# One v block turned on TensorE, paced loads, idle products and shared last-token products in an attention-then-MLP kernel

## The chip, the cores and the metric

The kernel runs on one core of one Trainium2 chip. The metric is device time in microseconds (us), and each quoted figure is the median of several executions of one program.

## The reference

Four batches of 6080 tokens and 256 channels go through a channel attention (the 256x256 score matrix is over channels, not tokens) and then through a two-layer MLP with a tanh gelu:

```python
qn = q / (np.linalg.norm(q, axis=1, keepdims=True) + 1e-06)      # q, k, v: (4, 6080, 256) f32
kn = k / (np.linalg.norm(k, axis=1, keepdims=True) + 1e-06)
s = kn.transpose(0, 2, 1) @ qn / tau                             # (4, 256, 256)
a = softmax(s)                                                   # cut: max, exp, sum
x = (v @ a).reshape(24320, 256)
h = x @ w_in                                                     # (24320, 2048)
g = 0.5 * h * (1.0 + np.tanh(c * (h + 0.044715 * h * h * h)))
return g @ w_out                                                 # (24320, 256) f32
```

## The kernel before

Phase one reads q and k of batch 0, and builds the score matrix G and the column sums. A short head computes the softmax and folds the attention matrix into w_in (`aw` = a @ w_in), so that the MLP can work straight on v. Then come 48 blocks (12 a batch, 512 tokens each, the twelfth 448). Block n computes its first layer from the turned v block `vT` while PE also does the output products `yp` of block n-1, and, a slice at a time, the score products of the next batch:

```python
for i in range(NP):                                   # 8 steps a block
    hp = pH.tile([128, 2, 512], FP32, tag="h", name="hp")
    for j in range(2):
        fc = 2 * i + j
        for cc in range(2):
            nc.tensor.matmul(hp[:, j, :cols], lhsT=aw[:, cc, fc * 128 : fc * 128 + 128],
                             rhs=vT[:, cc, :cols], start=cc == 0, stop=cc == 1)
    nc.scalar.activation(g[:, 2 * i : 2 * i + 2, :cols], hp[:, :, :cols], AF.Gelu_apprx_tanh)
    ...                                               # cut: more_aw
    if before is not None:
        h = i % 2
        y_part(before, i // 2, h * NP, h * NP + NP)   # 8 output products of one slot of 128 tokens
    next(fill, None)                                  # a slice of the next batch's scores
```

v arrives by a load from GpSimd's queue, cast to bf16, and is turned by four DMA transposes from SyncE's queue, one for each slot of 128 tokens. Block 1 is turned ahead of the loop, every later block two blocks ahead:

```python
def turn_v(nb):
    t = v_of.pop(nb)
    ...
    for s in range(n):
        nc.sync.dma_start_transpose(out=vT[:, :, s * 128 : s * 128 + 128], in_=t[:, s, :])
...
    vT = vT_of.pop(nb)          # in the loop over blocks
    turn_v(nb + 2)
    load_v(nb + 4)              # five buffers for v
```

Before the first block the kernel asks for both weight matrices, v blocks 1 to 3 and the first three q/k pieces of batch 1, in one burst. The twelfth block of a batch has 448 tokens: three full slots and one of 64. The half slot takes as many output products (16) as a full one:

```python
nc.tensor.matmul(yp[:rows, at, :], lhsT=g[:, fc, s * 128 : s * 128 + rows],
                 rhs=wout_bf[:, fc, :], start=fc == 0, stop=fc == FC - 1)
```

## Time and profile before

| | before |
|---|---|
| median of 3 runs | 776.29 us (775.14 to 776.45) |
| profiled execution | 776.96 us, span 775.2 us, mean granted clock 0.989 |
| PE busy | 95% of the span |
| PE waits for the turned v of block 1 | 10.1 us |
| block 0, 1, 2, 3 start | 45.03, 64.59, 81.63, 97.26 us |
| an ordinary block, from start to start | 15.20 to 15.63 us while it also does score products (blocks beside a change of batch differ), 13.89 us where it doesn't |

A block's start is read throughout as the start of its first weight load on PE; its first product begins up to 0.3 us later. The span runs from the first to the last instruction; device time is 1.8 us more. Two lines of the page's costliest groups show how to tell a bound engine from a waiting one (busy and mean duration come ahead of the second bar, idle time and what ended most of it after it):

```profile
L488 ACT ACTIVATE g<-hp 128x1024 bf16<-128x1024 f32 (+1 forms) x384 | 389.6, 1015 | 327.1 <-PE hp L484 307.6
L262 POOL DMA_DIRECT2D vb<-in_v_dram x47 | 25.5, 543 | 213.0 <-DMA vT<-vb 204.7
```

ScalarE stood idle 307.6 us for PE's products, so it follows PE. GpSimd stood 204.7 us for transposes to land before it could ask for another v block, which costs nothing by itself: it sits on a queue far ahead of need. Only a wait of PE is time lost.

### The profile page before, as it was taken

The numbers are of one execution on the slowest core, as the hardware profiler recorded it, in microseconds if no ns is written. First come the engines' busy times: TensorE is split into PE (matmuls) and PEld (weight loads), VectorE is DVE, ScalarE is ACT, GpSimd is POOL, SyncE is SP. The second block draws the span as 40 slices with busy tenths as digits, with TensorE's granted clock in tenths as the row PEclk, the third lists the DMA queues.
The fourth block names the chain that finished last, engine by engine and source line by source line (L and its number), as shares of the span: only waits on it lengthen the run. The fifth ranks groups of instructions, "written<-read, shape, count | busy, mean of one in ns | idle before, by whom it ended". The sixth has DMA issues, their size and how long they took to land.

```text
span 775.2 us, 12214 instructions
## 1 busy us (share of the span) xinstructions
PE 739.3 (95%) x5155; PEld 507.8 (66%) x5240; DVE 277.9 (36%) x487; ACT 420.9 (54%) x413; POOL 65.2 (8%) x121
## 2 busy tenths in 40 slices
PE   4776999999999999999999999999999999999998
PEld 3534666666666666666667666666766666666666
DVE  4731454544521454544431264545351101110011
ACT  5752555555555555555545555555545555555552
POOL 0231011001210001000300010100100000000000
PEclk9987999999999999999999999999999999999999
DMA  9999568412983365721695167723432333212111
GB/s 367 319 193 174 105 127 144 82 41 63 187 140 82 76 126 99 149 52 41 119 173 112 38 130 133 132 55 78 85 69 80 67 69 89 60 50 74 40 55 52
DMA packets 82039, 83.86 MB, mean 108 GB/s; under 512 B 56640, under 2 KB 61504, under 8 KB 81984
## 3 DMA queue, kind: packets, MB, share of 16 engines
q0 software_dynamic: 17648, 32.97, 25.8%
q1 hardware_dynamic: 64048, 49.18, 23.7%
q8 instruction: 41, 0.67, 0.4%
q10 hardware_dynamic: 288, 0.92, 0.3%
q14 instruction: 14, 0.11, 0.0%
HBM read 78.91 MB, written 24.90 MB: 134 GB/s over the span
## 4 chain that ended last, share of the span: by engine, by line
PE 90%; DMA 6%; SPq 1%; issue 1%; ACT 1%; POOL 0%; DVE 0%; ACTq 0%; DVEq 0%
PE yp L432 44%; PE hp L484 41%; PE G L124 4%; DMA st<-in_k_dram 3%; DMA vT<-vb 2%; DMA vb<-in_v_dram 1%; PE ps L184 1%; SPq L276 0%; POOL win_bf L291 0%; ACT sqb L230 0%; SPq L78 0%; PE cols L136 0%; ACT g L488 0%; PE T L162 0%; DVE qkb L225 0%
## 5 line engine op out<-in xcount | busy, mean ns | idle before, releaser
L488 ACT ACTIVATE g<-hp 128x1024 bf16<-128x1024 f32 (+1 forms) x384 | 389.6, 1015 | 327.1 <-PE hp L484 307.6
L484 PE MATMUL hp<-vT,aw 128*128 128x512 bf16 (+1 forms) x1458 | 385.4, 378 | 14.0 <-DMA vT<-vb 10.1
L432 PE MATMUL yp<-wout_bf,g 128*128 128x256 bf16 (+1 forms) x3072 | 397.9, 273 | 0.8 <-issue 0.2
L432 PEld LDWEIGHTS <-g 128*128 128x128 bf16 (+1 forms) x3072 | 301.1, 98 | 114.7 <-issue 3.3
L484 PEld LDWEIGHTS <-aw 128*128 128x128 bf16 x1536 | 149.8, 98 | 117.9 <-issue 14.5
L449 DVE COPY ysb<-yp 128x512 f32<-128x512 f32 (+1 forms) x93 | 64.0, 689 | 402.7 <-PE yp L432 402.7
L373 DVE TENSOR_TENSOR acc<-acc,sq 128x512 f32<-128x512 f32 (+1 forms) x141 | 97.5, 692 | 4.8
L124 PE MATMUL G<-qkb 128*128 128x256 bf16 (+1 forms) x384 | 74.0, 296 | 14.9 <-DVE qkb L225 14.9
L372 DVE TENSOR_TENSOR sq<-qkb 128x512 bf16<-128x512 bf16 (+1 forms) x141 | 58.7, 417 | 0.0
L124 PEld LDWEIGHTS <-qkb 128*128 128x128 bf16 (+1 forms) x384 | 39.0, 105 | 23.4 <-DVE qkb L225 15.8
L262 POOL DMA_DIRECT2D vb<-in_v_dram x47 | 25.5, 543 | 213.0 <-DMA vT<-vb 204.7
L193 DVE TENSOR_SCALAR aw<-ps,rsinv 128x512 bf16<-128x512 f32 x30 | 22.4, 749 | 26.2 <-PE ps L184 21.2
L78 POOL DMA_DIRECT2D qkb<-in_q_dram x24 | 13.2, 549 | 203.0 <-PE G L124 119.3
L230 ACT ACTIVATE sqb<-st 128x3072 bf16<-128x3072 f32 (+5 forms) x10 | 21.1, 2123 | 10.6 <-DMA st<-in_k_dram 10.6
L225 DVE CAST qkb<-st 128x3072 bf16<-128x3072 f32 (+6 forms) x12 | 14.6, 1225 | 15.0 <-DMA st<-in_k_dram 15.0
L184 PE MATMUL ps<-win_bf,eT 128*128 128x512 bf16 x54 | 17.1, 394 | 0.1
L383 POOL TENSOR_TENSOR r<-r,half 128x4 f32<-128x4 f32 x3 | 3.1, 1038 | 142.1 <-DVE r L382 142.1
L78 POOL DMA_DIRECT2D qkb<-in_k_dram x24 | 13.2, 549 | 4.5 <-DMA wout_bf<-in_moe_w_out_dram 1.9
L408 DVE RECIPROCAL den<-den 128x256 f32<-128x256 f32 x6 | 10.5, 1753 | 0.2
L453 DVE COPY ysb<-yp 64x256 f32<-64x256 f32 (+1 forms) x7 | 2.7, 415 | 21.2 <-PE yp L432 21.2
L184 PEld LDWEIGHTS <-eT 128*128 128x128 bf16 x60 | 5.9, 101 | 2.5 <-issue 1.1
L212 DVE TENSOR_TENSOR pair<-sqb 128x1536 bf16<-128x1536 bf16 (+2 forms) x7 | 5.8, 836 | 0.0
(51 smaller groups left out, 66.5 us busy)
## 6 DMA issues: line engine op xcount, KB each, us to landing
out_dram<-ysb SPq DMA_DIRECT2D x44, 512.0 KB, 2.9
vb<-in_v_dram POOLq DMA_DIRECT2D x43, 256.0 KB, 5.6
qkb<-in_q_dram POOLq DMA_DIRECT2D x21, 384.0 KB, 6.0
qkb<-in_k_dram POOLq DMA_DIRECT2D x21, 384.0 KB, 8.0
st<-in_q_dram SPq DMA_DIRECT2D x5, 768.0 KB, 10.4
st<-in_k_dram SPq DMA_DIRECT2D x5, 768.0 KB, 12.1
vT<-vb SPq DMA_TRANSPOSE x188, 3.8
out_dram<-ysb SPq DMA_DIRECT2D x4, 384.0 KB, 2.4
```

Source lines behind the costliest of these rows:

```text
L78: engines[x].dma_start(out=dst[:, x, 0:size, :], in_=src[b, s0 * 128 : (s0 + size) * 128, :].rearrange("(p s) c -> p s c", s=size))
L124: nc.tensor.matmul(G[:, ic, :], lhsT=qk[:rows, 1, s, ic * 128 : ic * 128 + 128], rhs=qk[:rows, 0, s, :], start=first and ic == 0, stop=las ...
L184: nc.tensor.matmul(ps, lhsT=eT[:, jc, ic * 128 : ic * 128 + 128], rhs=win_bf[:, jc, fs * 512 : fs * 512 + 512], start=jc == 0, stop=jc == 1)
L193: nc.vector.tensor_scalar_mul(dst, ps, scale)
L230: nc.scalar.activation(sqb[:rows, :, lo:hi], st[:rows, :, lo:hi], AF.Square)
L262: nc.gpsimd.dma_start(out=t[:, 0:n, :], in_=v_rows[r0 : r0 + n * 128, :].rearrange("(p s) c -> p s c", s=n))
L372: nc.vector.tensor_mul(sq[:rows], flat, flat)
L373: nc.vector.tensor_add(acc[:rows], acc[:rows], sq[:rows])
L432: nc.tensor.matmul(yp[:rows, at, :], lhsT=g[:, fc, s * 128 : s * 128 + rows], rhs=wout_bf[:, fc, :], start=fc == 0, stop=fc == FC - 1)
L449: nc.vector.tensor_copy(ysb[:, s0 : s + 1, :], yp[:, 0 : s + 1 - s0, :])
L484: nc.tensor.matmul(hp[:, j, :cols], lhsT=aw[:, cc, fc * 128 : fc * 128 + 128], rhs=vT[:, cc, :cols], start=cc == 0, stop=cc == 1)
L488: nc.scalar.activation(g[:, 2 * i : 2 * i + 2, :cols], hp[:, :, :cols], AF.Gelu_apprx_tanh)
```

## The change

Its intent has three parts. First, get rid of the wait at block 1: turn that v block on PE during block 0, and ask for less in the first burst (v block 3 ahead of the second q/k piece; four v buffers, not five). Second, keep the PE clock up through the tail of phase one and the softmax head by products on a constant `filler` tile that nobody reads. Third, let the half-full last tokens of two batches share one set of 16 output products, and spread a block's output products evenly over its steps. The core of the diff (cuts are marked):

```diff
-    vin = ctx.enter_context(tc.tile_pool(name="vin", bufs=5))
+    vin = ctx.enter_context(tc.tile_pool(name="vin", bufs=4))
...                                # cut: the last two phase-one chunks reuse free halves of earlier staging buffers
+    def keep_clock(n):
+        for _ in range(n):
+            idle = pH.tile([128, 2, 512], FP32, tag="h", name="idle")
+            nc.tensor.matmul(idle[:, 0, :], lhsT=filler[:, 0:128], rhs=filler, start=True, stop=True)
...
+        if n >= TAIL - 2:         # phase one, chunk n of 11 (TAIL = 7)
+            keep_clock(size)
...
-    for n in range(3):
-        load_qk(1, n)
-        if n < 2:
-            load_v(n + 2)
+    load_qk(1, 0)
+    load_v(2)                     # the rest is asked for from block 0 on
...
+    keep_clock(5)                 # head, ahead of turning the scores
...
-        nc.scalar.activation(vT0[:, cc, :], vps[:, cc, :], AF.Copy)    # in the loop over cc
+    nc.scalar.activation(vT0, vps, AF.Copy)
+    keep_clock(1)
...
-    turn_v(1)
+    def turn_v_on_pe(nb):
+        ...
+        for cc in range(2):
+            for s in range(4):
+                nc.tensor.matmul(p[:, cc, s * 128 : s * 128 + 128],
+                                 lhsT=t[:, s, cc * 128 : cc * 128 + 128],
+                                 rhs=ident_bf, is_transpose=True)
+        nc.vector.tensor_copy(vT, p)
...
+        for n in range(10):
+            if n % 3 == 0 and n < 9 and (b, n // 3) not in loaded_of:
+                load_qk(b, n // 3)
+            if b == 1 and n == 5:
+                turn_v_on_pe(1)
             yield
...
-            load_v(nb + 4)
+            load_v(nb + 3)
+            if cols % 128:        # the half slot
+                if kept is not None:
+                    gr, row0 = kept
+                    nc.gpsimd.tensor_copy(g[:, :, cols : cols + rest], gr)
+                    now["rests"] = [(0, row), (rest, row0)]
+                    now["rows"] = now["rows"] + [2 * rest]
+                elif b + 1 < B:
+                    gr = grp.tile([128, FC, rest], BF16, tag="gr", name="gr")
+                    kept = (gr, row)
...
-                    h = i % 2
-                    y_part(before, i // 2, h * NP, h * NP + NP)
+                    todo = [(s, fc) for s in range(len(before["rows"])) for fc in range(FC)]
+                    for s, fc in todo[len(todo) * i // NP : len(todo) * (i + 1) // NP]:
+                        y_part(before, s, fc, fc + 1)
+            if cols % 128 and kept is not None:
+                nc.gpsimd.tensor_copy(kept[0], g[:, :, cols - rest : cols])
```

More of the change, by code (lines that the diff above doesn't have):

```diff
@@ L54 @@
     gp = ctx.enter_context(tc.tile_pool(name="gp", bufs=2))
-    vin = ctx.enter_context(tc.tile_pool(name="vin", bufs=5))
+    vin = ctx.enter_context(tc.tile_pool(name="vin", bufs=4))
+    grp = ctx.enter_context(tc.tile_pool(name="grp", bufs=1))
     pA = ctx.enter_context(tc.tile_pool(name="pA", bufs=2, space=bass.MemoryType.PSUM))
@@ L89 @@
     n_all = S_ALL + 1
-    first_chunks = chunks_of([2, 5, 6, 6, 6, 6, 6, 4, 3, 2, 1], 7)
-    TAIL = 7
+    first_chunks = chunks_of([2, 5, 6, 6, 6, 6, 6, 4, 3, 2, 1], 1)
+    TAIL, SHARED = 7, 9
     staged = []
@@ L97, in stage_chunk @@
         if n < len(first_chunks):
-            st = stage.tile([128, 2, SMAX, 256], FP32, tag="st", name="st")
+            if n < SHARED:
+                st = stage.tile([128, 2, SMAX, 256], FP32, tag="st", name="st")
+            else:
+                st = staged[n - 2][:, :, first_chunks[n - 2][1] :, :]
             load_chunk((nc.sync, nc.scalar if n < 2 else nc.sync), st, 0, first_chunks[n])
@@ L106 @@
     make_identity(nc, ident)
+    ident_bf = const.tile([128, 128], BF16)
+    nc.gpsimd.tensor_copy(ident_bf, ident)
+    filler = const.tile([128, 512], BF16)
+    nc.gpsimd.memset(filler, 1.0)
     ones_bf = const.tile([128, 1], BF16)
@@ L348 @@
     vT_of[0] = vT0
-    turn_v(1)
-    def attention_steps(b, aw_next):
-        if b > 1:
-            for n in range(3):
-                load_qk(b, n)
-        for _ in range(10):
+    def turn_v_on_pe(nb):
+        t = v_of.pop(nb)
+        vT = vts.tile([128, 2, 512], BF16, tag="vT", name="vT")
+        p = pA.tile([128, 2, 512], BF16, tag="a", name="vps")
+        for cc in range(2):
[4 more added lines that the diff above has]
+        nc.vector.tensor_copy(vT, p)
+        vT_of[nb] = vT
+    def attention_steps(b, aw_next):
+        for n in range(10):
[3 more added lines that the diff above has]
+                turn_v_on_pe(1)
             yield
@@ L446, in y_part @@
         s0 = s - at
-        n = sum(x == 128 for x in rows_of)
+        n = st["n"]
         if s < n:
@@ L456, in y_part @@
                 out=out[r0 : r0 + n * 128, :].rearrange("(p s) c -> p s c", s=n), in_=ysb[:, 0:n, :])
-        if s >= n:
-            nc.sync.dma_start(out=out[r0 + n * 128 : r0 + n * 128 + rows, :], in_=ysb[:rows, s, :])
+        for lo, row in st["rests"] if s >= n else []:
+            nc.sync.dma_start(out=out[row : row + rest, :], in_=ysb[lo : lo + rest, s, :])
+    rest = N % 128
+    assert rest <= 64
+    kept = None
     before = None
@@ L472 @@
             turn_v(nb + 2)
-            load_v(nb + 4)
+            load_v(nb + 3)
             g = gp.tile([128, FC, 512], BF16, tag="g", name="g")
+            n_full = cols // 128
             now = {
                 "b": b, "blk": blk, "g": g, "final": nb == B * n_blocks - 1,
-                "rows": [min(128, cols - s * 128) for s in range((cols + 127) // 128)],
+                "n": n_full, "rows": [128] * n_full, "rests": [],
             }
+            if cols % 128:
+                row = b * N + t0 + n_full * 128
+                if kept is not None:
[3 more added lines that the diff above has]
+                    now["rows"] = now["rows"] + [2 * rest]
+                    kept = None
+                elif b + 1 < B:
+                    gr = grp.tile([128, FC, rest], BF16, tag="gr", name="gr")
+                    kept = (gr, row)
+                else:
+                    now["rests"] = [(0, row)]
+                    now["rows"] = now["rows"] + [rest]
             for i in range(NP):
```

## The prediction

> **What bounds the kernel now.** I read the page first (engine shares, then the chain that ended last), then busy time by stretch, then the timeline at the one gap, then the waits and the landings around that gap. The page:
>
> ```profile
> span 775.2 us, 12214 instructions
> PE 739.3 (95%) x5155; PEld 507.8 (66%) x5240; DVE 277.9 (36%) x487; ACT 420.9 (54%) x413; POOL 65.2 (8%) x121
> PE 90%; DMA 6%; SPq 1%; issue 1%; ACT 1%; POOL 0%; DVE 0%; ACTq 0%; DVEq 0%
> L432 PE MATMUL yp<-wout_bf,g 128*128 128x256 bf16 (+1 forms) x3072 | 397.9, 273 | 0.8 <-issue 0.2
> ```
>
> PE is the bound, and 90% of the chain is its products. What is to be had is either fewer products or the 6% of DMA. A step of the steady part, from the PE timeline (pairs of rows: four first-layer products, then eight output products):
>
> ```profile
> 640.81 1.04 PE L432 MATMUL yp<-wout_bf,g 128*128 128x256 bf16 x8
> 641.69 1.03 PE L484 MATMUL hp<-vT,aw 128*128 128x512 bf16 x4
> 642.55 1.04 PE L432 MATMUL yp<-wout_bf,g 128*128 128x256 bf16 x8
> ```
>
> Starts are what counts, since the modelled ends overlap: a group of either kind takes 0.87 us (641.69 to 642.55), so an output product costs 0.1085 us and a step 1.735 us. The gap, by stretches:
>
> ```profile
> 37.00:46.50 9.50, 7.31 (x29) 4.29 (x31) 4.38 (x11) 5.28 (x10) 5.06 (x9) 0.64 1.10 166
> 54.50:64.60 10.10, 0.04 (x1) 0.00 (x1) 0.69 (x1) 1.10 (x2) 3.33 (x7) 0.71 1.12 204
> 64.60:100.00 35.40, 34.94 (x228) 23.29 (x234) 14.89 (x28) 17.41 (x17) 3.21 (x7) 0.94 0.80 128
> ```
>
> Columns: stretch, length, busy time of PE, PEld, DVE, ACT, POOL, then granted clock, DMA share, GB/s. PE does nothing for 10.1 us while DMA is full (1.12). The chain and the waits say for what:
>
> ```profile
> 37.03 9.48 DMA vb<-in_v_dram
> 50.44 14.06 DMA vT<-vb
> 64.63 1.44 PE hp L484 x3
> ...
> PE hp L484 <- DMA vT<-vb: 10.1, 1, 10.1
> ```
>
> v block 1 is loaded by 46.51, then turned by four DMA transposes, the last of which lands at 64.49. The landings of block 1's and of block 2's transposes (from issue, min/median/max):
>
> ```profile
> DMA to landing us min/median/max: 8.0/10.4/14.1
> ...
> DMA to landing us min/median/max: 8.1/12.2/15.0
> ```
>
> From load landed to last transpose landed is 18.0 us for block 1 (46.51 to 64.49) and 17.9 us for block 2 (60.55 to 78.44), where the whole-trace median of one transpose is 3.8 us. Block 2 starts on PE at 81.74, only 3.3 us after its own transposes. This is what I rest the prediction on.
>
> **What the Trainium skill says.** "DMA: Bandwidth & Descriptors", Queues, rings and completion order: an engine goes round-robin between its queue rows and drains a whole packet of one before it turns to the next. The trace agrees: between 55 and 63 us the transposes get some 60 of their 256 B packets per us beside load packets of 2 to 3 KB (about 240 ns each), and over 400 in single microseconds after the loads have run dry. "TensorE: Matmul & The Clock Gate", Part 1: the PE clock falls to half after an idle window of about 3.4 us and returns after a busy one. The trace agrees: the grant is 0.50 from 58.8 to 69.0 us, 4.2 us after PE fell idle. Same page, Part 4: transpose-mode products do not count as busy for that gate; before has four on Gs and eight on v0 from 38.3 us, and the grant is 0.50 from 38.28 to 45.1. No run shows yet whether the cause is the transposes or the 1.4 us idle ahead of them.
>
> **The change, part by part.**
> 1. v block 1 on PE: eight bf16 transposes and a DVE copy of 128x1024 put into block 0, in place of four DMA transposes. Its load landed at 46.51, so it can run at about 51. Cost on PE: at most eight times 0.1 us (estimate from 0.1085 us for 256 columns), partly behind ACT, which sets the last steps of block 0 (1.02 us per gelu against 0.87 us). It removes the 10.1 us and the cold restart: two first-layer groups and one output group take 64.63 to 69.36, 4.7 us in place of 3 x 0.87 = 2.6, so 2.1 us. Together 12.2 us, if nothing else waits.
> 2. Loads: the third v block is asked for ahead of the second q/k piece, and v has four buffers, not five. POOL waits only for landings and freed buffers, not for PE, so this reorders the loads; v block 2 keeps its place as twelfth load. But the fifth v load now waits for block 2's transposes. So the first burst is 6592 - 512 = 6080 KB (from the issue table: weights 2048, v blocks 1 to 4 in place of 1 to 6, q/k 3008).
> 3. Idle products: 22 behind the first-phase chunks and 6 in the softmax head. In the tail of phase one PE is nearly full (6.44 of 7.5 us in 29.5 to 37), and ten of them stand in it at 0.217 us, so I give them +0.8 us there. In the head (38.28 to 45.29), if the clock stays up, the ten or so 512-column products and twelve transposes save about 2 us, limited by the second weight piece (landed 42.35). One merged vT copy takes out a wait of 0.7 us. Net: block 0 starts near 44, not 45.29. The earlier last chunks (no buffer wait) gain little past that, since DVE and ACT then set the tail.
> 4. Shared last tokens: batches 0 and 2 lose one slot of 16 output products each: 32 x 0.1085 = 3.5 us, all on the path, since ACT is idle 0.7 us a step there. Two copies on POOL lie beside. At the very end one output DMA becomes two: +0.5 us (an issue takes 0.51).
>
> **Where block 2 lands.** PE alone would reach it at 44 + 9.6 (block 0: 9.26 before, plus transposes) + 15.0 (block 1: 8 x 1.735 + 5 q/k pairs x 0.218) = 68.6. Its v still comes by DMA transposes. The load lands about 59 (60.55 less the 1.5 us that block 1's transposes took of the engines), and its transposes would take 18 us beside loads, to 77, unless the loads run dry. They ran dry at 78.1 after 42.1 us for 6592 KB; 512 KB less is 3.3 us, and 1024 transpose packets of 30 ns on 16 engines less is 1.9 us: 72.9, and the last landing 73.5. So I expect PE to wait about 5 us at block 2: the wait moves one block on. Gain there: 81.74 - 73.5 = 8.2 us. A wait of 5 us probably spans an idle window: +1.3 us of cold restart (2.1 times a chance of about 0.6).
>
> **Sum.** -8.2 + 1.3 - 3.5 + 0.5 = -9.9 us: 776.3 becomes 766.4. Points 1 and 3 of the head are inside the 8.2: earlier arrival only lengthens the wait.
>
> **The rivals.**
> (a) The wait is gone altogether, as the loads are light enough for block 2's transposes by 68.6. For it: block 2's first two transposes landed after 8 to 10 us. Against it: its last two took 14 to 15. Then the gain is 81.74 - 68.6 = 13.1, plus 3.0: 760.2, just over 2%.
> (b) The wait is not smaller but longer: full 18 us after the load, 77, with a cold restart: gain 4.7 - 2 + 3 = 5.7, so 770.6.
> (c) Idle products hold PE behind in phase one by 2 us or more, because six of them run cold (0.43 us each, 2.6 us) ahead of chunk 5. In my main case the wait at block 2 hides this; in (a) it shows, 762.
> (d) POOL's copies or the four v buffers stall a later block. Against: the instruction lists have PE waiting for POOL only one block after each copy, and v loads lead by about two blocks of 15 us. Under 1 us.
>
> **Range and chances.** Most weight lies on block 2 starting between 70 and 76, which gives 761 to 771.5. The 2% line is 760.8; even with no wait at all I come out only just below it, so faster has 0.10; the shared products alone make slower nearly impossible, 0.02.
>
> **What would show it.** Right: a PE wait of 3 to 7 us for DMA vT at about 69 us with DMA share above 1; block 2's first products near 73.5; 32 output products fewer, with the three-slot blocks' successors 1.7 us shorter; no wait at block 1. Wrong: no PE wait for vT at all (then 760 or less), a granted clock of 0.5 through the head as before, first-phase sums ending after 38.5 us, or a new PE wait at a batch boundary (about 235 or 600 us).

## The result

| | before | after |
|---|---|---|
| median (4 runs each) | 776.32 us (775.14 to 776.45) | 764.08 us (762.57 to 764.33) |
| ratio of after to before | | 0.9842, 95% interval 0.9825 to 0.9859 |
| span of the profiled execution | 775.2 us | 760.8 us, clock 0.998 |

A ratio is the mean time of one kernel's runs over that of the other's in the same rounds, so it isn't quite the ratio of the two medians. The change took 12.2 us, 1.6%, off the time; the prediction was 766.4 us. The interval of the ratio stays clear of 1. Note that the profiled execution of after was also its fastest one (762.57 us, the other three took 763.92 to 764.33).

The page of after:

```profile
span 760.8 us, 12295 instructions
PE 737.9 (97%) x5240; PEld 503.1 (66%) x5240; DVE 277.9 (37%) x486; ACT 420.2 (55%) x412; POOL 70.0 (9%) x127
PE 90%; issue 4%; DMA 4%; POOL 1%; SPq 0%; DVE 0%; POOLq 0%
L462 PE MATMUL yp<-wout_bf,g 128*128 128x256 bf16 x3040 | 393.3, 273 | 0.0
```

There are 3040 output products in place of 3072, and the "+1 forms" of before is gone: no 64-column product is left, since four half slots of 16 products became two full ones. (PE's total of records is no guide to this: before's trace lacks some, 5155 products beside 5240 weight loads.) PE's share rose from 95 to 97%. The third line (the chain of work that ended last) is a trap for the reader: DMA's 6% became 4% and a new 4% of "issue" appeared, but the chain of after simply tells the first 31 us, the loads of phase one, as one piece of "issue", where before told most of that as a DMA. So it doesn't show the gain. What does is the busy time by stretch (stretch, length; busy time of PE, PEld, DVE, ACT, POOL; granted clock, DMA share, GB/s):

```profile
37.00:46.50 9.50, 8.92 (x77) 5.44 (x76) 4.36 (x11) 5.79 (x9) 5.78 (x10) 1.00 1.14 164
...
54.50:64.60 10.10, 10.01 (x70) 6.75 (x70) 2.68 (x6) 6.07 (x7) 1.80 (x4) 1.00 1.09 199
64.60:100.00 35.40, 33.28 (x236) 22.62 (x235) 17.28 (x33) 17.55 (x18) 3.71 (x7) 1.00 0.93 152
```

The stretch in which PE did nothing is now full (10.01 of 10.10), the head runs at clock 1.00 in place of 0.64, and 2.1 us are missing from the last stretch (33.28 of 35.40). The waits and the PE timeline say where:

```profile
PE hp L534 <- DMA vT<-vb: 2.1, 1, 2.1
```

```profile
69.36 0.38 PE L140 MATMUL G<-qkb 128*128 128x256 bf16 x2
71.86 1.02 PE L534 MATMUL hp<-vT,aw 128*128 128x512 bf16 x4 [2.12 <-DMA vT<-vb]
72.72 1.04 PE L462 MATMUL yp<-wout_bf,g 128*128 128x256 bf16 x8
```

and the chain follows the wait back to the load of v block 2 and the last of its four transposes:

```profile
44.61 10.91 DMA vb<-in_v_dram
...
59.44 12.28 DMA vT<-vb
71.72 0.14 issue
71.86 1.02 PE hp L534 x4
```

The wait moved one block on and shrank. Where the rest came from is seen in the blocks' lengths. A block with a half slot does its three full slots and the half one while the next block runs, so the successors of the short blocks are the ones to look at (their start, to the start two blocks on, because weight loads run a little ahead of the products there):

| stretch | before | after | difference |
|---|---|---|---|
| start of block 2 | 81.63 | 71.83 | -9.80 |
| block 2 | 15.63 | 15.55 | -0.08 |
| blocks 12 and 13 | 29.32 | 27.14 | -2.2 |
| blocks 24 and 25 | 29.32 | 28.87 | -0.45 |
| blocks 36 and 37 | 28.23 | 26.04 | -2.2 |
| block 47 to the end | 24.20 | 24.50 | +0.30 |

These sum to -14.4 us, which is the difference of the two spans (775.2 to 760.8); every other block has the same length in both to 0.01 us. In after a successor of a three-slot block has steps of four first-layer and six output products, 1.52 us apart in place of 1.735:

```profile
224.33 1.03 PE L534 MATMUL hp<-vT,aw 128*128 128x512 bf16 x4
225.20 0.82 PE L462 MATMUL yp<-wout_bf,g 128*128 128x256 bf16 x6
225.85 1.03 PE L534 MATMUL hp<-vT,aw 128*128 128x512 bf16 x4
```

### The profile page after: what moved, and what is told of

It is laid out like the page before. It is cut to its first block, busy times and chain, and to the rows that moved or that the text cites. A ratio compares the mean times of both kernels' runs of the same rounds, so it can differ in the third digit from the quotient of the medians.

```text
span 760.8 us, 12295 instructions
## 1 busy us (share of the span) xinstructions
PE 737.9 (97%) x5240; PEld 503.1 (66%) x5240; DVE 277.9 (37%) x486; ACT 420.2 (55%) x412; POOL 70.0 (9%) x127
## 4 chain that ended last, share of the span: by engine, by line
PE 90%; issue 4%; DMA 4%; POOL 1%; SPq 0%; DVE 0%; POOLq 0%
PE yp L462 43%; PE hp L534 41%; PE G L140 4%; DMA vT<-vb 2%; DMA vb<-in_v_dram 1%; PE ps L200 1%; DMA win_bf<-in_moe_w_in_dram 1%; SPq L294 0%; POOL win_bf L309 0%; PE cols L152 0%; PE T L178 0%; POOL filler L116 0%; DVE ysb L483 0%; POOL ident masks.py:199 0%; POOL ident_bf L114 0%
## 5 line engine op out<-in xcount | busy, mean ns | idle before, releaser
L462 PE MATMUL yp<-wout_bf,g 128*128 128x256 bf16 x3040 | 393.3, 273 | 0.0
L534 PE MATMUL hp<-vT,aw 128*128 128x512 bf16 (+1 forms) x1536 | 390.6, 377 | 2.4 <-DMA vT<-vb 2.1
L462 PEld LDWEIGHTS <-g 128*128 128x128 bf16 x3040 | 296.8, 98 | 113.6
L140 PE MATMUL G<-qkb 128*128 128x256 bf16 (+1 forms) x384 | 71.7, 288 | 15.7 <-DVE qkb L241 15.7
L241 DVE CAST qkb<-st 128x3072 bf16<-128x3072 f32 (+6 forms) x12 | 14.6, 1224 | 15.3 <-DMA st<-in_k_dram 15.3
L519 POOL COPY g<-gr 128x1024 bf16<-128x1024 bf16 x2 | 2.1, 1037 | 104.5 <-PE yp L462 104.5
L547 POOL COPY gr<-g 128x1024 bf16<-128x1024 bf16 x2 | 2.1, 1034 | 87.6 <-ACT g L538 87.6
L136 PE MATMUL idle<-filler 128*128 128x512 bf16 x28 | 7.5, 385 | 0.0
```

Of the source, the lines that this page charges most:

```text
L140: nc.tensor.matmul(G[:, ic, :], lhsT=qk[:rows, 1, s, ic * 128 : ic * 128 + 128], rhs=qk[:rows, 0, s, :], start=first and ic == 0, stop=las ...
```

## The experiments

All kernels gave correct results and were timed against before in the same rounds; a ratio is always to before. Three calls and a last single kernel went to four different chips, whose medians of before were 776.7, 777.3, 776.81 and 776.46 us.

### Is the spread of after its own? (after_again)

The kernel is after, unedited.

> The changed kernel once more, to see how far its time and its wait at block 2 move from run to run (the profiled run was at 762.6 us, the other three at 763.9 to 764.3). Mine (the wait moved to block 2's transposes, whose end follows from when the load burst runs dry): 763 to 765 us, a PE wait of 1.5 to 4 us for DMA vT near 70 us, block 2's first products at 71.8 to 73.5. Rival (the 1.5 us between runs come from the PE clock in the head, not from DMA): block 2 starts at the same time within 0.3 us and the granted clock differs before 46 us.

Measured: 763.86 us (762.09 to 765.17), ratio 0.9835 (0.9819 to 0.9852). Its profiled execution was the slow end of these (765.17), and its PE timeline differs from after's at block 2:

```profile
67.79 0.38 PE L140 MATMUL G<-qkb 128*128 128x256 bf16 x2
71.84 1.87 PE L534 MATMUL hp<-vT,aw 128*128 128x512 bf16 x4 [3.67 <-DMA vT<-vb]
73.51 1.91 PE L462 MATMUL yp<-wout_bf,g 128*128 128x256 bf16 x8
```

PE came 1.6 us sooner than in after (the last product ahead of the wait starts a group at 67.79 in place of 69.36), yet block 2 began at the same time, 71.84 against 71.86. That is what a DMA bound looks like: an earlier arrival only lengthens the wait. And after 3.7 us of idling the group of four took 1.67 us to the next start (71.84 to 73.51) in place of 0.86: the clock records show 0.5 from 70.6 to 77.4 us. Block 3 began at 90.00, against 87.38 in after, where the 2.1 us wait cost no clock. So this cold restart cost 2.6 us here, and it comes in some executions and not in others: the run of 762.09 us has a mean granted clock of 1.000, so it had none. The Trainium skill ("TensorE: Matmul & The Clock Gate", Part 1) says that the activity window is free-running. Two traces of one kernel that differ so fit with it, but don't show it, since the waits differ too: 2.1 us and no drop in one, 3.7 us and 6.8 us at half clock in the other. Waits of 3.5 us in v1_pe_only and no_idle below were followed by 3.4 us at half clock, and cost about 1.5 us each.

### The shared products alone (shared_only)

Edit, to before: the shared last tokens and the even spread, with loads, buffers and turning as before.

```diff
+                    gr = grp.tile([128, FC, rest], BF16, tag="gr", name="gr")
+                    kept = (gr, row)
...
-                    y_part(before, i // 2, h * NP, h * NP + NP)
+                    for s, fc in todo[len(todo) * i // NP : len(todo) * (i + 1) // NP]:
+                        y_part(before, s, fc, fc + 1)
```

> The kernel before with the shared last tokens and the even spread alone. Prediction's sum (32 products x 0.1085 us, less 0.5 us at the end): 3.0 us gained, 773.3. Mine after seeing the trace: the half slots cost more than their products, because PE stalls where 128-column weights change to 64-column ones and back (0.54 us a slot in the blocks that follow the short ones), so 2 x 2.28 + 2 x 0.54 - 0.3 - 0.3 = 5.0 us, less what the next block gives back: 4.3 to 5.0 us gained, 771.5 to 772. Rival (the later part of the gain has another source, such as fewer stalls at batch changes): 3.0 to 3.5.

Measured: 772.29 us, ratio 0.9949 (0.9936 to 0.9961), so about 4.0 to 4.4 us. Its blocks 12 to 13, 24 to 25 and 36 to 37 are as long as after's, to 0.02 us, so all of that part of the gain belongs to the sharing with its even spread. The three together are 4.8 us; 32 products removed at 0.1085 us are only 3.5 us. The end gives back 0.5 us here (24.72 us against 24.20). The time lies a little above the 771.5 to 772 us that was expected.

### Why a removed half slot is worth more than its products (full_width)

Edit, to before: the half slot is multiplied at full width, over a zeroed rest, so it has as many products but no 64-column weights:

```diff
-                yp[:rows, at, :],
-                lhsT=g[:, fc, s * 128 : s * 128 + rows],
+                yp[:, at, :],
+                lhsT=g[:, fc, s * 128 : s * 128 + 128],
...
+            if cols % 128:
+                nc.gpsimd.memset(g[:, :, cols:512], 0.0)
```

> The kernel before with the half slot's weights loaded 128 columns wide (the upper 64 are zeros written by POOL and their products are thrown away): same number of products, no change of width. If the change of width costs 0.54 us a slot: 4 slots, 1.5 to 2.2 us gained (the last one stands at the end and changes width once), block 12 at 13.89 us in place of 14.43. If the price is the number of products only: no change, and POOL's memset may cost a little.

Measured: 775.11 us, ratio 0.9982 (0.9970 to 0.9994): computing twice as many columns is faster, by 1.4 to 1.6 us. The PE timelines of the last two steps of block 12, first before, then full_width:

```profile
244.64 1.03 PE L484 MATMUL hp<-vT,aw 128*128 128x512 bf16 x4
245.59 1.06 PE L432 MATMUL yp<-wout_bf,g 128*64 128x256 bf16 x8
246.59 1.04 PE L484 MATMUL hp<-vT,aw 128*128 128x512 bf16 x4
247.55 1.06 PE L432 MATMUL yp<-wout_bf,g 128*64 128x256 bf16 x8
248.55 1.04 PE L484 MATMUL hp<-vT,aw 128*128 128x512 bf16 x4
```

```profile
244.69 1.03 PE L486 MATMUL hp<-vT,aw 128*128 128x512 bf16 x4
245.55 1.04 PE L432 MATMUL yp<-wout_bf,g 128*128 128x256 bf16 x8
246.43 1.03 PE L486 MATMUL hp<-vT,aw 128*128 128x512 bf16 x4
...
248.16 1.03 PE L486 MATMUL hp<-vT,aw 128*128 128x512 bf16 x4
```

Two steps take 3.91 us before (244.64 to 248.55) and 3.47 us at full width (244.69 to 248.16). A mean duration doesn't show it: by form, the 64-column output products of before have 275 ns each and the 128-column ones 273. It lies in the starts: each group ahead of or behind a change of width takes 0.95 or 1.00 us in place of 0.87, some 0.11 us a change, and four changes make 0.44. The blocks 24 and 25 of after agree: no product is removed there, only the width is changed, and they take 28.87 us, as in full_width (28.88), in place of 29.32. On the weight-load row the same shows as idle time that has no releaser:

```profile
245.59 0.79 PEld L432 LDWEIGHTS <-g 128*64 128x64 bf16 x8 [0.42 <-issue]
246.58 0.55 PEld L484 LDWEIGHTS <-aw 128*128 128x128 bf16 x4 [0.20 <-issue]
```

The weight loads stop at the change and don't run ahead of the products. The Trainium skill ("TensorE: Matmul & The Clock Gate", Part 2, Weight-path perf modes) says that the fast weight load is on when the number of weights is 128 and the type isn't FP32. The trace agrees so far that a 64-column load isn't faster than a 128-column one (109 ns against 98 by form). Whether the stop comes from that mode or from the output's 64 rows, which changed with it, isn't told apart here.

### Block 1 on PE alone (v1_pe_only)

Edit, to before: block 1 is turned on PE in block 0; the order of the loads and the five buffers stay. But the edit does more than its name says, and the expectation didn't count it: the load of v block 6, the last of before's burst, was asked for at 65.05 us there and is asked for at 74.80 us here, after GpSimd waited 15.3 us for block 2's transposes. So the burst is 256 KB lighter too.

```diff
-    turn_v(1)
+            if b == 1 and n == 5:
+                turn_v_on_pe(1)
```

> The kernel before with v block 1 turned on PE, all loads as before. Mine (loads' end sets block 2): 6592 KB in place of 6080 KB before block 2's transposes get through, so block 2 starts about 3 us later than in the changed kernel, at 74 to 76 us, PE waits 4 to 6 us there, perhaps with a cold restart; gain over before 5 to 8 us, 768 to 771. Rival (the reordering and the buffer count do not matter, the number of transposes does): block 2 at 71.9 as in the changed kernel, gain 9 to 10 us, 766 to 767.

Measured: 769.08 us, ratio 0.9902 (0.9887 to 0.9917). The wait is at block 2 here too, 3.5 us, and its last transpose lands at 74.25:

```profile
46.03 10.85 DMA vb<-in_v_dram
...
60.81 13.44 DMA vT<-vb
74.25 0.14 issue
74.38 1.86 PE hp L499 x4
```

In before that landing is at 78.44, in after at 71.72. So block 1's four transposes and one v block of 256 KB, taken off the DMA engines together, are worth 4.2 us at block 2. What after changes beyond that (another v block out of the burst, the new order, the staging of phase one) is worth 2.5 us, and isn't taken apart. The load of v block 2 shows the transposes by themselves, since the same loads stand ahead of it in both kernels: it was asked for at 45.65 and 46.03 us, and landed at 60.55 in before and at 56.88 here, 3.7 us sooner.

### A lighter burst (light_burst), and its repeat (light_again)

If the loads that stand beside block 2's transposes set its start, then asking for one q/k piece (768 KB by the issue table, q and k together) later must remove the wait. The edit puts it behind the fifth v load, which waits for block 2's transposes: it was asked for at 68.98 us in place of 55.22. Edit, to after:

```diff
-            load_qk(b, n + 3)
+            if b == 1 and n == 1:
+                load_qk(1, 3)
+            if not (b == 1 and n == 0):
+                load_qk(b, n + 3)
```

> The changed kernel with one pair of loads moved: the fourth q/k piece of batch 1 (768 KB) is asked for after the fifth v load, so the first burst is 5312 KB in place of 6080. Theory (block 2 starts when the burst has run dry and its transposes get through): dry about 4.7 us earlier, near 65.5 us, transposes landed near 67, so no PE wait at block 2, which then starts when PE gets there, 68.0 to 69.6 us; with no wait there is no cold restart either. Gain over the changed kernel 2 to 6 us: 758.5 to 762. Rival (block 2's transposes are slow for a reason of their own, such as their issue or the transpose path): wait as before, block 2 at 71.8, 764.

Measured: 758.98 us (758.80 to 760.49), ratio 0.9772 (0.9758 to 0.9786). The first burst is 5312 KB in place of 6080, its last load lands at 66.84 us, block 2's last transpose at 67.90, and PE doesn't wait for it at all:

```profile
67.91 0.38 PE L140 MATMUL G<-qkb 128*128 128x256 bf16 x2
68.12 1.03 PE L537 MATMUL hp<-vT,aw 128*128 128x512 bf16 x3
```

> The lighter burst once more, on the same chip as the next two, to compare with: 758.5 to 760.5 us, no PE wait after block 0, block 0 at 42.5 to 44.5.

Measured, the same kernel on another chip: 758.94 us, ratio 0.9777 (0.9764 to 0.9790). It repeats.

### The same wait removed the other way (v12_pe)

Edit, to after: block 2 is turned on PE as well, in block 1, and the loads stay.

```diff
-            turn_v(nb + 2)
+            if nb != 0:
+                turn_v(nb + 2)
...
+                if nb == 1 and i == 4:
+                    turn_v_on_pe(2)
```

> The changed kernel with v block 2 turned on PE as well, in the middle of block 1. Theory: the wait at block 2 is gone at the price of eight bf16 transposes (0.44 us in block 0): block 2 at 68.5 to 70.1, 759 to 762.5. Rival (the wait moves one block on once more, to block 3's transposes, 85.4 us): block 3 later than 85.4. I expect no such wait, since v block 3's load lands near 57 us and the burst is dry by 71.

Measured: 759.61 us, ratio 0.9776 (0.9763 to 0.9789). Block 2 began at 68.54 and nothing waited; block 3's transposes, which landed at 73.22, were in time. Two different cures, one by the queue and one by PE, give the same time, so the wait at block 2, with the cold restart behind it where it comes, is the 5 us or so by which after falls short of them.

### The idle products (no_idle, light_no_idle, light_head_idle, light_mid_idle)

no_idle is after without any of them:

```diff
-        if n >= TAIL - 2:
-            keep_clock(size)
...
-    keep_clock(5)
...
-    keep_clock(1)
```

> The changed kernel without any of the 28 idle products. Theory: the first phase's sums end near 37 us in place of 37.9 to 39.5, the head then runs at a granted clock of 0.5 as in the kernel before and takes back what was won, so block 0 starts at 44.5 to 45.5; block 2 still starts at 71.8 because DMA sets it: 762.5 to 765, the same as the changed kernel within 0.3%. Rival (the idle products are worth their 6.8 us of half clock): block 0 at 46 or later and 766 to 767.

Measured: 763.80 us, ratio 0.9830 (0.9814 to 0.9846), against 0.9835 of after_again: no difference. Block 0 began at 42.58, the wait at block 2 was 3.5 us with a cold restart behind it, block 2 at 71.33. But after's wait would hide a loss of up to some 2 us in the head, so the test that counts is on the light burst, which has no wait to hide it:

> The lighter burst without any idle product: here no wait at block 2 hides what they are worth. In the run without them the head ran warm all the same, so theory: they gain nothing that can be relied on; when the clock stays up, block 0 starts at 42.6, when it drops, at 44.5 to 45.5, which moves the time with it: 758.5 to 762, spread over 2 us between runs. Rival (they pay): every run cold in the head, 761 to 762, and 2 to 3 us slower than the lighter burst.

Measured: 759.44 us, ratio 0.9779, in the same rounds as light_again's 758.94 and 0.9777. Block 0 began at 42.52 and 42.66. The idle products gain nothing that can be measured.

light_head_idle keeps only the six in the head, light_mid_idle only the first twelve of phase one's tail and the head's:

```diff
-        if n >= TAIL - 2:                  # light_head_idle takes these two lines out
+        if TAIL - 2 <= n < TAIL:           # light_mid_idle
             keep_clock(size)
```

> The lighter burst, and idle products in the softmax head alone (6), none behind the chunks (22 less). Theory: in the first phase's tail PE is bound, so 10 idle products there cost 0.8 to 2.6 us; without them the sums end near 37 us, the head still runs warm, block 0 starts near 42.3 (second weight piece landed at 41.0 to 41.9), and block 2 near 67.5 with a wait of at most 1 us: 756.5 to 760. Rival (the products behind the chunks are needed to keep the clock up): the granted clock is 0.5 in the head, block 0 at 44 to 45, no better than the lighter burst alone.

Measured: 760.11 us, ratio 0.9781 (0.9767 to 0.9794), beside light_burst's 758.98 of the same rounds. Its profiled execution ran cold until 35.9 us and waited 1.0 us at block 2. The 1.1 us is inside the intervals.

> The lighter burst with idle products behind chunks 5 and 6 and in the head, none behind the last four chunks (10 fewer, 0.217 us each): if these ten stand in PE's way in the tail, the sums end 0.8 to 1.5 us earlier (36.5 to 37.1 us) and the time falls by as much, to 757.5 to 758.5. Rival: the tail is set by DVE and ACT, or the clock drops without them: no gain.

Measured: 758.54 us, ratio 0.9770 (0.9757 to 0.9783), beside 758.94 of light_again: the lowest median of all, but no difference that the intervals allow. Its profiled execution still waited 0.4 us at block 2, so the lighter burst is only just light enough.

### The merged copy in the head (light_split_copy)

Without idle products the head still ran at full clock in no_idle and light_no_idle, and in before it didn't. One thing that differs there is the copy of the turned block 0, once in two halves and once merged. Edit, to light_no_idle:

```diff
-    nc.scalar.activation(vT0, vps, AF.Copy)
+        nc.scalar.activation(vT0[:, cc, :], vps[:, cc, :], AF.Copy)     # in the loop over cc
```

> The lighter burst without idle products, and with block 0's vT copy split in two again as in the kernel before (PE's second four transposes then wait for ACT's first copy, 1.0 us). Theory: it is this wait, together with the 1.4 to 1.7 us ahead of the Gs transposes, that let the clock drop in the head of the kernel before (all three traces with the split copy and a warm start have a granted clock of 0.5 from 38 to 40 us on, none with the merged copy has): granted 0.5 for 3.4 to 6.8 us there, block 0 at 44 to 45.3, time 760.5 to 762 against 759.4 with the merged copy. Rival (the drop is chance, or comes from the DMA-turned v block): clock stays at 1.0 and only the wait of 0.7 us shows: 759.5 to 760.3.

Measured: 761.52 us (759.54 to 762.77), ratio 0.9799 (0.9781 to 0.9817), 2.1 us above light_no_idle; the intervals overlap. It was run on another chip. The split copy's own cost shows in the waits:

```profile
PE vps L330 <- ACT vT L333: 0.7, 1, 0.7
```

But the profiled execution, the slowest of the five, didn't lose its clock in the head: it never had it. Two groups of twelve products of 256 columns, from its PE timeline in phase one and in full clock from light_burst's:

```profile
30.73 2.74 PE L140 MATMUL G<-qkb 128*128 128x256 bf16 x12 [2.04 <-DVE qkb L241]
```

```profile
30.70 1.48 PE L140 MATMUL G<-qkb 128*128 128x256 bf16 x12 [1.75 <-DVE qkb L241]
```

2.74 us against 1.48 for the same twelve. The clock column of the stretches says 1.00 for both, since that trace's clock records begin only at 46.7 us with the rise to full; the durations are what to go by. So block 0 began at 47.10 for a reason that lies ahead of the edit. The run shows the 0.7 us and no more; whether the split copy makes the clock drop in the head is open. For it speaks that three profiled kernels with the split copy entered the head at full clock and lost it there (before, shared_only, v1_pe_only) and that all nine with the merged copy kept it; but those nine differ in other things too.

## Why the prediction was right

**The bound and the mechanism.** It held that PE is the bound, that the wait at block 1 goes, and that it comes back at block 2 because block 2's transposes still stand beside the loads. All three are shown: the two profiles of after wait for the turned v at block 2 and nowhere else; block 2 began at 71.8 us in both though PE came 1.6 us apart; and taking loads away (light_burst) or the transposes (v12_pe) removes the wait. That the transposes land when the burst runs dry, on which the sum rests, shows in four profiles: the last load of the burst and block 2's last transpose landed at 78.09 and 78.44 us in before, 73.61 and 74.25 in v1_pe_only, 70.96 and 71.72 in after, 66.84 and 67.90 in light_burst. Rival (a), no wait at all, is what those two kernels made real: 759 and 760 us, where (a) had put 760.2.

**Where block 2 lands: right in kind, 1.8 us too late.** The prediction had the last landing at 73.5 us; it was 71.72 (71.71 in the repeat). Its sum had two terms for the earlier end of the burst, 3.3 us for 512 KB and 1.9 us for block 1's transposes: 5.2 us, where the burst ended 7.1 us earlier. The transposes were mis-sized: without them the load of v block 2 landed 3.7 us sooner in v1_pe_only, where the prediction had taken 1.5 us off it. So their packets' own 30 ns aren't all that they cost. In after that load, put at about 59 us, landed at 55.52, 10.9 us after its issue in place of 14.9. Whether the cost lies in the interleaving at the engines wasn't measured by itself, and the term for the 512 KB has no run of its own.

**The length of the wait.** About 5 us was expected, 3 to 7 as the mark of being right; measured 2.1 and 3.7. Only the repeat's lies inside the mark. PE's arrival, put at 68.6, was near 69.7 in one profile and 68.2 in the other.

**The cold restart: right as a chance.** The working gave 2.1 us times 0.6. Where it came, it cost 2.6 us (after_again) or about 1.5 us (v1_pe_only and no_idle, where half clock lasted half as long). Three of four runs of after lie 1.35 us or more above its fastest, which was the profiled one that had no drop; that most runs do restart cold is thus likely, but only profiles show it: one of after's two, v1_pe_only's and no_idle's.

**Shared products: 3.5 us predicted, 4.8 measured in the blocks.** This is the other mis-sized term of the sum. It counted products and not the changes between 128 and 64 columns of weights, 0.45 us at each of the three half slots inside the loop (the fourth is part of the end). full_width shows it alone.

**The end.** +0.5 us predicted for two output transfers in place of one, +0.30 measured in after and +0.52 in shared_only. v1_pe_only, whose end is that of before, differs from before by 0.25 us itself, so the sign is shown and the size roughly.

**The idle products.** The tail of phase one did end later: the last column sums began at 39.42 us in after's profile, against 36.66 before, beyond the 38.5 that the prediction had named as a mark of being wrong; in the repeat they ended near 38.0. The 39.42 belongs to an execution whose granted clock was 0.5 from 30.7 to 34.1 us. no_idle had the same drop (31.0 to 34.4), and its last column sums began at 37.27: so there the idle products held PE back by some 2.1 us, as rival (c) feared, and the wait at block 2 hid it, as the prediction had said. On the light burst their medians show no effect, but neither profile of it with all 28 had such a drop. Block 0 began at 44.43 and 42.87 us, near the 44 predicted. That the clock in the head needs these products to stay up is refuted: it stayed up without them in no_idle and in light_no_idle.

**The sum.** In the repeat's profile, with the restart of 2.6 us, the blocks give -9.8 + 2.6 - 4.8 + 0.3 = -11.7 us; in after's, without a restart, -14.4; the medians give -12.2. The prediction had -8.2 + 1.3 - 3.5 + 0.5 = -9.9. Against the repeat, two gains were undersized by 1.6 and 1.3 us and one loss by 1.3, and the end was put 0.2 too dear: 1.8 us in the blocks. The path was right; that the times lie only 2.3 us apart (766.4 and 764.08) is partly luck, as a loss put too small offset gains put too small. Rival (d), a stall at a later block by GpSimd's copies or the four buffers, isn't seen in any trace: all other blocks keep their length, and the copies of 1.03 us have no one waiting for them.

## What to carry to other kernels

When one wait for a transfer is removed, look at once for the next buffer on the same queue: here the wait simply came one block later, and asking for 768 KB some 14 us later gained another 5 us. The version to keep is the light burst without the idle products, which gained nothing measurable: 759.44 us, 2.2% under before. Where PE is the bound, try to keep the number of weight columns the same from product to product (a change cost 0.11 us here); padding a half slot with zeros to full width was faster than skipping the columns, and sharing the slot was better still. And judge a clock remedy on a kernel where no wait lies behind it to hide what it does.

## What the Trainium skill lacked or had wrong

- "TensorE: Matmul & The Clock Gate", Part 2: no cost is given for changing between 128 and 64 columns of weights. Here it is some 0.11 us a change, 0.45 us for a half slot (two steps in 3.91 us against 3.47). Its formula for a weight load, columns over 1.2, gives 53 ns for 64 columns; the trace has 109 ns for 64 and 98 ns for 128.
- The same page, Part 2, Back-to-back issue gap: it gives about 131 ns as the sustained spacing of 512-column products in a real kernel and calls N / 2.4 + 2.5 ns too long there. Here four such products, each with its weight load, take 0.87 us from start to start, 0.217 us each, which is that formula's 216 ns.
- The same page, Part 4: it gives about 275 ns as the duration of one transposing product in a kernel's context, and no spacing of several. Here one has 273 to 278 ns in f32 and 219 ns in bf16 by form (after), but eight bf16 ones of 128x128 take 0.44 us from the first start to the next group's (52.01 to 52.45 us in after), 0.055 us each. That such products don't count as busy couldn't be confirmed: the head's twelve ran at full clock in every profiled execution that entered the head with it, except in before, shared_only and v1_pe_only, which also have the split copy and its wait of PE.
- The same page, Part 1: the warm-up is told as about 3.4 us of sustained work, without how much of that time must be busy. Work with gaps of 0.72 us in every 3.8 us (17 to 28 us) wasn't at full clock until 46.7 us in one profiled execution (light_split_copy), and was by 17 to 22 us in six others of nearly the same program.
- "DMA: Bandwidth & Descriptors" has no figure for how much a DMA transpose is slowed beside a burst of loads: 12.0 us from issue to landing in the middle here (block 2 of after) against 3.9 us over the whole trace. Nor has it one for how much they slow the loads: without four of them the next v load landed 3.7 us sooner (v1_pe_only).
